# Sliding attention beside a dense block: attention from the last tile to the first, WO blocks in other slots, results turned in place

## The chip, the cores and the metric

The kernel runs on one core of one Trainium2 chip. The metric is the time of one execution on the device in microseconds (us), as the median of several runs. TensorE is PE, VectorE DVE, ScalarE ACT, GpSimd POOL, and SyncE, which here only issues DMAs, SP.

## The reference

One input x of 2048 rows and 576 columns is normed and goes through an attention and a dense block side by side; both are added to x:

```
x  = A_x                                   # 1 x 2048 x 576
xn = layernorm(x)
A: q, k, v = split(xn @ wqkv)              # 32 heads of 18
   key of position s, window place w:  s - 2 w, w = 0..7   (none below 0)
   o = softmax(q . k * 18**-0.5) . v;  o @ wo
B: relu(xn @ w1) @ w2                      # w1 576 x 4608, w2 4608 x 576
out = x + A + B
```

All is float32. Each operand is cut into a high and a low part, and a product is the sum of three partial products.

## The kernel before, in words

**Phases.** The dilation is 2, so even and odd rows never meet. The kernel treats them as two phases (`ph` 0 and 1) of 1024 rows. A partition holds eight consecutive rows of its phase, the tiles 0 to 7 (`NI`): the attention of tile i is that of the i-th row of all 128 partitions.

**The dense block** fills PE. Its first part goes slot by slot (24 slots per phase; slots of phase 1 are counted from 1000): `h_two` makes hidden values, 1.5 us of PE, and `o_two` multiplies them by W2. Its larger part goes by groups (`group`, 30 per phase), in which two by two blocks are multiplied with Strassen's seven products. A group has eight steps; after each step's products (place "T") and after the half output pass behind them (place "O"), `fire` runs what was put at that place by `on(ph, group, step, place, ...)`. The cuts of the weights are such events: `sw_load` and `sw_prep` (W1; A11, S1, ... are its blocks), `w2_load` and `w2_split` (W2), `wq_load` and `wq_split` (the QKV weights). A cut copies the high part on ACT (L172) and subtracts on DVE (L176) or POOL (L174).

**Attention** goes by four units (`u`) of eight heads. `qkv_half` (L488) makes Q, K and V of a unit on PE; ACT puts them into rows of one tile, `att` (L520): Q, K and V each have row numbers there, and V and Q have two places, for even and odd units. `halos` (L527) copies the last seven rows of the partition before to the first seven rows of K and V, by DMAs on SP (L533). `attention` (L542) then queues a list of small jobs: for each tile a product with the window of eight keys (`qk_mul`, L563) and its sum (`qk_sum`, L566), the softmax (`sm_max`, L575, and on), the values (`av_mul`, `av_add`), `o_turn` (L607), which transposes the result block by block, and `o_out`, which writes it to memory with eight DMAs. Tile i reads rows i to i + 7 of K and V; rows 0 to 6 are the halo. After one of the sums POOL masks the places below position 0 (`affine_select`, L569), in partition 0.

**Which job runs when** is settled while the program is written. `run_bg(margin)` (L645) takes jobs from the list as long as the planner's count of DVE time stays within `margin` of its count of PE time. So the jobs stand at fixed places among the cuts and ReLUs on DVE, and each engine takes its instructions in that order.

**WO.** When a phase's last unit is written, `ot_plan` (L1092) says in which order and with which spacing WO is loaded and cut (`wl`, `ws`) and the results are read back and cut (`in`, `split`), on the planner's count of PE time. `wo_block` (L1235) multiplies 256 rows by WO. Block 0 of phase 0 ends `seam`, between the phases; blocks 1 to 3 run in slots 1003, 1006 and 1009 of phase 1, behind `h_two`. Their operands lie in the memory that phase 1's `att` takes over, so phase 1's first `wq_load` (slot 1010) can be issued only when they are through.

**The second phase's x** is normed in phase 0's last slots: `xq_load`, `stats`, `xq_norm`, `turn`, and `blocks_out` (L387, DMAs at L391), which writes the turned tile to memory.

Places in the queue lists: `at(n, ...)` runs in slot n ahead of the output pass, `late(n, ...)` behind it. DMAs on SP go in order of the program.

## Time and profile before

| | us |
|---|---|
| median of 3 runs | 1171.43 (1170.77 to 1171.69) |
| the profiled execution | 1176.77 |
| its span on the core | 1175.0 |
| PE busy | 1125.7 (96%) |
| DVE busy | 816.7 (70%) |
| ACT busy | 562.2 (48%) |
| POOL busy | 472.7 (40%) |

The profile is of one execution. The mean granted PE clock was 0.984 of full speed. A name such as "PE po L163 <- DVE ar L176" says that an instruction of line 163 on PE, which writes tile po, stood idle until DVE's instruction of line 176 on tile ar was done; a line may be that of a helper, so that many places share it. SPq is SP's queue of DMA issues.

### The profile page before, as it was taken

The numbers are of one execution on the slowest core, as the hardware profiler recorded it, in microseconds if no ns is written. First come the engines' busy times: TensorE is split into PE (matmuls) and PEld (weight loads), VectorE is DVE, ScalarE is ACT, GpSimd is POOL, SyncE is SP. The second block draws the span as 40 slices with busy tenths as digits, with TensorE's granted clock in tenths as the row PEclk, the third lists the DMA queues.
The fourth block names the chain that finished last, engine by engine and source line by source line (L and its number), as shares of the span: only waits on it lengthen the run. The fifth ranks groups of instructions, "written<-read, shape, count | busy, mean of one in ns | idle before, by whom it ended". The sixth has DMA issues, their size and how long they took to land.

```text
span 1175.0 us, 38355 instructions
## 1 busy us (share of the span) xinstructions
PE 1125.7 (96%) x16410; PEld 1103.4 (94%) x16410; DVE 816.7 (70%) x1249; ACT 562.2 (48%) x1316; POOL 472.7 (40%) x514
## 2 busy tenths in 40 slices
PE   8999899999999999999997999999999999999996
PEld 8998899999999999998997999999999999999895
DVE  7675788698798788874315438877896886888431
ACT  4443463454355455556534235635644634555540
POOL 2323452353354355553323135434524523555331
PEclk9999899999999999999999999999999999999898
DMA  7479795786697598899947157858858957888984
GB/s 217 156 170 197 139 196 91 142 173 118 141 184 129 98 185 140 156 184 281 189 63 157 24 106 169 157 86 174 173 95 160 204 92 164 143 155 155 215 131 111
DMA packets 159810, 176.82 MB, mean 150 GB/s; under 512 B 36232, under 2 KB 107144, under 8 KB 159608
## 3 DMA queue, kind: packets, MB, share of 16 engines
q0 software_dynamic: 44352, 81.45, 47.5%
q1 hardware_dynamic: 114604, 92.03, 26.8%
q8 instruction: 129, 2.11, 0.7%
q10 hardware_dynamic: 684, 0.88, 0.2%
q14 instruction: 41, 0.34, 0.1%
HBM read 74.07 MB, written 95.70 MB: 144 GB/s over the span
## 4 chain that ended last, share of the span: by engine, by line
PE 73%; DMA 12%; DVE 6%; issue 3%; ACT 3%; SPq 2%; POOL 1%; DVEq 0%; ACTq 0%; POOLq 0%
PE po L163 23%; PE po L142 19%; PE ph L163 12%; PE pm L163 10%; PE pm L142 5%; DMA st<-in_w 4%; DMA out<-ev 3%; PE ph L142 3%; DVE ar L176 2%; DMA att<-od 1%; DMA att<-att 1%; ACT ev L711 1%; DMA xS<-od 1%; DMA od<-pr 1%; DVE ar L757 1%
## 5 line engine op out<-in xcount | busy, mean ns | idle before, releaser
L163 PE MATMUL po<-ar 64*128 64x320 f32 (+1 forms) x5760 | 475.6, 292 | 7.0 <-DVE ar L176 6.3
L163 PEld LDWEIGHTS po<-ar 64*128 64x128 f32 x5760 | 414.9, 186 | 11.3 <-DVE ar L176 9.0
L724 POOL DMA_DIRECT2D out<-ev x256 | 226.6, 1026 | 399.3 <-ACT ev L711 373.0
L163 PE MATMUL ph<-xT,ar 64*128 64x256 f32 x2520 | 328.7, 279 | 15.6 <-ACT pm L975 7.5
L163 PEld LDWEIGHTS ph<-xT,ar 64*128 64x128 f32 x2520 | 291.8, 187 | 21.9 <-ACT pm L975 12.3
L711 ACT ACTIVATE ev<-po 128x512 f32<-128x512 f32 (+1 forms) x268 | 172.8, 650 | 218.2 <-PE po L163 110.4
L163 PE MATMUL pm<-xS,ar 64*128 64x256 f32 x2160 | 267.9, 279 | 1.8 <-ACT u L979 0.7
L163 PEld LDWEIGHTS pm<-xS,ar 64*128 64x128 f32 x2160 | 242.3, 187 | 3.7 <-DVE ar L757 1.1
L176 DVE TENSOR_TENSOR ar<-st,ar 128x256 fp32r<-128x256 f32 (+3 forms) x232 | 146.1, 641 | 64.2 <-ACT ar L172 54.3
L172 ACT ACTIVATE ar<-st 128x256 fp32r<-128x256 f32 (+3 forms) x304 | 147.9, 500 | 21.5 <-DMA st<-in_w 16.2
L174 POOL TENSOR_TENSOR ar<-st,ar 128x256 fp32r<-128x256 f32 (+1 forms) x72 | 94.3, 1323 | 158.6 <-ACT ar L172 156.7
L907 POOL TENSOR_TENSOR st<-st 128x256 f32<-128x256 f32 x120 | 135.9, 1145 | 12.1 <-DMA st<-in_w 7.8
L142 PE MATMUL po<-wq,xT 64*128 64x432 f32 x1296 | 136.4, 353 | 0.0
L142 PEld LDWEIGHTS po<-wq,xT 64*128 64x128 f32 x1296 | 123.6, 184 | 1.5
L163 PE MATMUL ph<-xS,ar 64*128 64x256 f32 x720 | 103.2, 276 | 1.0 <-ACT ph L975 0.8
L563 DVE TENSOR_TENSOR pr<-att 128x1152 f32<-128x1152 f32 x64 | 89.3, 1399 | 18.4 <-DMA att<-att 18.2
L598 DVE TENSOR_TENSOR pr<-att 128x1152 f32<-128x1152 f32 x64 | 89.9, 1423 | 12.2 <-ACT att L520 11.9
L163 PEld LDWEIGHTS ph<-xS,ar 64*128 64x128 f32 x720 | 94.0, 184 | 2.6 <-ACT ph L975 2.0
L566 DVE TENSOR_REDUCE att<-pr 128x64 f32<-128x1152 f32 x64 | 84.9, 1338 | 0.0
L142 PE MATMUL po<-ar 64*128 64x256 f32 (+1 forms) x984 | 73.1, 293 | 2.7 <-ACT ev L711 2.7
L757 DVE SCALAR_TENSOR_TENSOR ar<-u,ar 128x256 fp32r<-128x256 f32 x60 | 31.7, 528 | 63.2 <-ACT ar L753 63.1
L605 DVE TENSOR_TENSOR pr<-pr 128x1152 f32<-128x1152 f32 x64 | 71.5, 1117 | 1.4
(120 smaller groups left out, 1356.4 us busy)
## 6 DMA issues: line engine op xcount, KB each, us to landing
out<-ev POOLq DMA_DIRECT2D x268, 288.0 KB, 6.2
st<-in_w SPq DMA_DIRECT2D x72, 288.0 KB
st<-in_w SPq DMA_DIRECT2D x120, 128.0 KB
att<-att SPq DMA_DIRECT2D x16, 441.0 KB
att<-in_wqkv SPq DMA_DIRECT2D x28, 216.0 KB
od<-pr SPq DMA_DIRECT2D x32, 128.0 KB
att<-in_x SPq DMA_DIRECT2D x14, 288.0 KB
st<-in_w SPq DMA_DIRECT2D x60, 64.0 KB
```

Source lines behind the costliest of these rows:

```text
L142: ins = nc.tensor.matmul(o, l[z], r[z], start=start, stop=stop)
L163: b.ins = nc.tensor.matmul(b.ap, l[part], r[part], start=start, stop=stop, skip_group_check=skip)
L172: nc.scalar.activation(hi, src, AF.Copy)
L174: nc.gpsimd.tensor_tensor(lo, src, f32(hi), op=ALU.subtract)
L176: nc.vector.tensor_tensor(lo, src, f32(hi), op=ALU.subtract)
L563: nc.vector.tensor_tensor(pr[i], q, window(k, i), op=ALU.mult)
L566: nc.vector.tensor_reduce(lg[:, i], pr.pop(i).rearrange(heads, d=Dh), axis=AX.X, op=ALU.add)
L598: nc.vector.tensor_tensor(pr[i].rearrange(heads, d=Dh), e, window(v, i).rearrange(heads, d=Dh), op=ALU.mult)
L605: nc.vector.tensor_tensor(o, z[:, :, 0:n], z[:, :, n : 2 * n], op=ALU.add)
L711: nc.scalar.activation(acc[:, :, cols], z[:, :, 0 : cols.stop - cols.start], AF.Copy)
L724: ADDED[ph, 2 * tb + k] = nc.gpsimd.dma_start(o_v[ph, 2 * tb + k], acc[:, k, :], accum_op=ALU.add)
L907: nc.gpsimd.tensor_tensor(stg(o), stg(a), stg(b), op=op)
```

## The change

Seven things are changed. (1) The products and sums of attention run from tile 7 to tile 0, and the mask follows the sum of tile 0; attention starts one step later. (2) `o_turn` writes into the unit's own V rows and no longer into a scratch tile, and the list isn't held for 5 us behind `o_out` any more; in odd units ACT writes V in an instruction of its own. (3) The cut of A11 moves from step 3 to step 4. (4) WO is cut later behind its load. (5) WO block 1 moves ahead of the hidden pass of its slot, blocks 2 and 3 both ahead of slot 1006, and phase 1's first `wq_load` to slot 1008. (6) `blocks_out` goes behind the loads of its slot, and the statistics, norm and turn of the last two tiles move into groups 0 and 1. (7) Two margins of the list are smaller.

```diff
@@ qkv_half
-            assert len(bg) <= 26, (ph, u, len(bg))
+            assert len(bg) <= 30, (ph, u, len(bg))
...
-            nc.scalar.activation(
-                a[:, q0 + j : q0 + j + 2 * step + 1 : step, :], pq.rearrange("p (s c) -> p s c", s=3), AF.Copy
-            )
+            pq = pq.rearrange("p (s c) -> p s c", s=3)
+            for m, n in ((0, 2), (2, 3)) if u % 2 else ((0, 3),):
+                to = q0 + j + m * step
+                nc.scalar.activation(a[:, to : to + (n - m - 1) * step + 1 : step, :], pq[:, m:n, :], AF.Copy)
@@ attention
         def qk_mul(i):
-            if i % 2 == 0:
+            if i % 2:
                 both = prp.tile([P, 2, W, UD], F32, name="pr")
-                pr[i], pr[i + 1] = both[:, 0], both[:, 1]
+                pr[i], pr[i - 1] = both[:, 0], both[:, 1]
...
-            if i == NI - 2:
+            if i == 0:
                 z = lg[0:1, 0 : NI - 1]
                 nc.gpsimd.affine_select(
...
         def o_turn():
-            z = pr["o"] = prp.tile([P, 5, NI, 32], F32, name="pr")
+            k = V_ROW[u % 2] * UD
+            z = pr["o"] = att(ph)[:, k : k + 5 * NI * 32].rearrange("p (g i e) -> p g i e", g=5, e=32)
...
-            hold["bg"] = t["pe"] + 5.0
...
-        for i in range(0, NI, 2):
+        for j in (NI - 1, NI - 2):
             for f in (qk_mul, qk_sum):
-                for j in (i, i + 1):
+                bg.append((big, f, (j,)))
+        for i in range(NI - 3, 0, -2):
+            for f in (qk_mul, qk_sum):
+                for j in (i, i - 1):
                     bg.append((big, f, (j,)))
@@ run_bg
-        if t["pe"] < hold.get("bg", 0.0):
-            return
@@ plan_strassen
-                on(ph, a - 1, 3, "T", sw_prep, ph, p, "A11")
+                on(ph, a - 1, 4, "T", sw_prep, ph, p, "A11")
...
-            on(ph, g + 2, 2, "O", attention, ph, u)
+            on(ph, g + 2, 3, "O", attention, ph, u)
@@ ot_plan
-            z.append((("ws", kt), wo_split, (ph, kt), None, (("wl", 6 + 1.4 * (kt - 2)),)))
+            z.append((("ws", kt), wo_split, (ph, kt), None, (("wl", 12 + 2.0 * (kt - 2)),)))
...
-            z.append((("in", r), ot_in, (ph, r), free if r == 3 else done, ((("in", r - 1), 5.0),) if r else (("wl", 5.0),)))
+            z.append((("in", r), ot_in, (ph, r), free if r == 3 else done, ((("in", r - 1), 5.0),) if r else (("wl", 6.0),)))
@@ prologue
-        run_bg(1.0)
+        run_bg(0.3)
@@ new
+    def wo_third():
+        EV[0, 3, "wo"] = prp.tile([P, 2, D], F32, name="pr"), []
+        wo_block(0, 3)
@@ phase 0, tiles of the second phase
-                late(n + 1 + odd, do)
                 if i < 6:
+                    late(n + 1 + odd, do)
                     late(n + 2 + odd, xq_norm, i)
                     late(n + 2 + odd, turn, xq(i), 1, i)
-                    at(n + 4, blocks_out, xq(i), 1, i)
+                    late(n + 4, blocks_out, xq(i), 1, i)
                 else:
-                    on(0, 0, 2 + 3 * odd, "O", xq_norm, i)
-                    on(0, 0, 2 + 3 * odd, "O", turn, xq(i), 1, i)
-                    on(0, 0, 7 + odd, "O", blocks_out, xq(i), 1, i)
+                    on(0, 0, 1 + 4 * odd, "O", do)
+                    on(0, 1, 2 + 3 * odd, "O", xq_norm, i)
+                    on(0, 1, 2 + 3 * odd, "O", turn, xq(i), 1, i)
+                    on(0, 1, 5 + 3 * odd, "O", blocks_out, xq(i), 1, i)
@@ phase 1, first slots (first() runs ahead of h_two)
-            for r in range(1, NTB):
-                at(b + 3 * r, wo_block, 0, r)
-            at(b + 10, wq_load, ph, 0)
+            first(b + 3, wo_block, 0, 1)
+            first(b + 6, wo_block, 0, 2)
+            first(b + 6, wo_third)
+            at(b + 8, wq_load, ph, 0)
...
-        late(b + UNIT0[ph] + NI + 1, attention, ph, 0)
+        late(b + UNIT0[ph] + NI + 2, attention, ph, 0)
@@ slots
-            run_bg(margin(n))
+            run_bg(margin(n) - (1.4 if n == b + NOLD - 4 else 0.0))
```

More of the change, by code (lines that the diff above doesn't have):

```diff
@@ L1343, in at, with first @@
         todo.setdefault(n, []).append((f, a))
+    todo_first = {}
+    def first(n, f, *a):
+        todo_first.setdefault(n, []).append((f, a))
     todo_late = {}
@@ L1521, in tile_body @@
             g = n - n % 2 + LAG
+            for f, a in todo_first.pop(n, []):
+                f(*a)
             if n < ROW0:
```

## The prediction

> **What bounds the kernel now.** The page comes first: which engine fills the span.
>
> ```profile
> span 1175.0 us, 38355 instructions
> PE 1125.7 (96%) x16410; PEld 1103.4 (94%) x16410; DVE 816.7 (70%) x1249; ACT 562.2 (48%) x1316; POOL 472.7 (40%) x514
> ```
>
> PE is the bound: it is busy for all but 49.3 us. The edits keep the matrix work; both built programs hold the same matmuls, DVE, POOL and DMA instructions, and ACT alone has 32 more. A gain can come only from PE's idle time and from the half-clock stretches behind it. So the second view is who PE waited for (total us, times, longest):
>
> ```profile
> PE ph L163 <- ACT pm L975: 7.5, 14, 1.8
> PE po L163 <- DVE ar L176: 6.3, 7, 1.6
> PE pm L142 <- ACT wq L172: 6.0, 1, 6.0
> PE ph L163 <- DVE ar L176: 5.5, 3, 4.8
> PE po L142 <- ACT ev L711: 2.7, 4, 1.3
> ```
>
> No releaser is slow by itself: the rows below show copies and splits of 0.4 to 0.6 us. Something holds its queue. The third view cuts the span around each stall (window, length, busy us of PE, PEld, DVE, ACT, POOL, then granted clock, DMA share, GB/s):
>
> ```profile
> 108.00:116.00 8.00, 7.07 (x102) 6.36 (x99) 4.22 (x5) 4.59 (x11) 3.17 (x4) 1.00 0.99 169
> 116.00:120.67 4.67, 0.00 (x2) 0.01 (x2) 3.57 (x11) 0.00 (x0) 2.38 (x4) 0.68 0.36 113
> 120.67:126.00 5.33, 5.11 (x47) 4.65 (x47) 3.60 (x7) 1.19 (x3) 2.56 (x4) 0.64 1.07 178
> 223.00:226.70 3.70, 1.84 (x24) 1.33 (x22) 3.70 (x5) 0.87 (x3) 0.44 (x1) 1.00 0.87 162
> 226.70:232.00 5.30, 5.30 (x66) 5.30 (x64) 4.64 (x8) 2.47 (x7) 1.78 (x2) 0.68 0.69 145
> 320.00:322.20 2.20, 1.63 (x21) 1.10 (x19) 2.20 (x4) 0.66 (x2) 0.42 (x1) 1.00 0.96 145
> 415.00:418.00 3.00, 1.30 (x15) 0.80 (x14) 3.00 (x5) 0.92 (x3) 0.95 (x1) 1.00 0.99 179
> 418.00:423.00 5.00, 5.00 (x60) 5.00 (x60) 4.44 (x7) 2.41 (x6) 1.68 (x2) 0.66 0.99 266
> 526.00:531.00 5.00, 2.82 (x36) 2.24 (x36) 3.14 (x5) 3.57 (x8) 1.96 (x3) 0.97 1.09 304
> 531.00:536.00 5.00, 5.00 (x62) 5.00 (x62) 1.27 (x3) 2.94 (x7) 2.24 (x3) 0.69 1.12 253
> 638.00:644.16 6.16, 0.17 (x2) 0.00 (x0) 2.20 (x5) 1.28 (x4) 0.00 (x0) 0.94 0.82 188
> 644.16:652.00 7.84, 7.84 (x69) 7.55 (x71) 7.38 (x13) 3.04 (x7) 1.97 (x2) 0.62 0.15 42
> 700.00:706.00 6.00, 4.78 (x61) 3.88 (x60) 5.03 (x8) 2.27 (x7) 2.86 (x4) 1.00 0.95 163
> 803.00:805.00 2.00, 0.91 (x11) 0.39 (x7) 2.00 (x4) 0.47 (x2) 0.41 (x1) 1.00 0.98 165
> 989.00:992.00 3.00, 1.30 (x16) 0.78 (x14) 3.00 (x5) 0.66 (x2) 1.22 (x1) 1.00 0.90 153
> 1100.00:1105.00 5.00, 2.51 (x30) 1.85 (x28) 3.09 (x5) 4.09 (x9) 1.77 (x2) 0.92 1.07 305
> 1105.00:1112.00 7.00, 7.00 (x72) 7.00 (x74) 2.56 (x6) 3.46 (x8) 2.64 (x3) 0.57 1.11 269
> ```
>
> Read them in pairs. A stall costs its idle time (length less PE busy) and then the work lost at the lower clock, (1 - clock) x length of the row behind it. Six stalls have a half-clock stretch behind them: the rows at 120.67, 226.70, 418, 531, 644.16 and 1105.
>
> **The change part by part**, each with the price of the stall that it touches.
>
> *Statistics of the second half, and the order on SP.* The DVE row shows the wait in brackets, the SP row the queue ahead of the load:
>
> ```profile
> 103.18 9.96 SPq L391 DMA_DIRECT2D words<-att  x8
> 116.96 0.82 DVE L303 BATCH_NORM_STATS2 bst<-att 128x6 f32<-128x288 f32 x2 [4.75 <-DMA att<-in_x]
> ```
>
> Eight block writes stood ahead of the load of x tiles 6 and 7, DVE waited 4.75 us for it, and the weight splits behind waited too. Now the loads go ahead of the block writes, and the statistics move into groups 0 and 1, behind those splits. The loads can be issued from 103.18 on, no longer behind 103.18 + 9.96 = 113.14; with the 3.8 us to landing seen before (116.96 - 113.14) they are there well ahead of 116. The 5.60 us idle in the first two windows and (1 - 0.64) x 5.33 = 1.92 go: 7.5. Late next are the splits of A22 and the remainder, about due when PE arrives; I keep 0.5 of cost there. Gain **7.0**.
>
> *Attention from the last tile, one step later.* Tile 7's window covers rows 7 to 14, its partition's own; the halo fills rows 0 to 6. In the changed program the first product waits for no DMA, the second for the halo. Before, the first one waited:
>
> ```profile
> 217.13 3.21 SPq L533 DMA_DIRECT2D att<-att  x4
> 222.75 1.92 DVE L563 TENSOR_TENSOR pr<-att 128x1152 f32<-128x1152 f32 x1 [3.94 <-DMA att<-att]
> 224.59 0.81 DVE L176 TENSOR_TENSOR ar<-st,ar 128x256 fp32r<-128x256 f32 x2
> ```
>
> The second split of L176, that of W2, held up PE at 223; the same happened at 320, 415, 803 and 989. In the new order it precedes attention. The second product comes about four and a half steps after the halo's issue, at the code's STEP of 1.46 us some 6.5 us; the halo took 222.75 - 217.13 = 5.6. Idle: 1.86 + 0.57 + 1.70 + 1.09 + 1.70 = 6.92; clock: 0.32 x 5.30 + 0.34 x 5.00 = 3.40. Of 10.3 I take **9.5**.
>
> *The seam.* WO blocks 2 and 3 now run back to back ahead of slot 1006, and the next QKV weights are issued in slot 1008 and no longer 1010. Their memory is free only when the last WO block is through, so SP waited for it.
>
> ```profile
> 575.43 1.53 PE pm L142 x26
> 576.97 1.59 PE po L142 x24
> ```
>
> The first row is one hidden pass, the second one output pass: together a slot of 3.1 us. WO block 3 moves from inside slot 1009 to ahead of slot 1006, past three slots and one hidden pass: 10.8 us earlier. The rows behind it were these:
>
> ```profile
> 624.36 2.58 SPq L229 DMA_DIRECT2D att<-in_wqkv  x4
> 630.06 0.86 SPq L207 DMA_DIRECT2D st<-in_w  x1
> 642.88 0.78 ACT L172 ACTIVATE ar<-st 128x256 fp32r<-128x256 f32 x2 [6.97 <-DMA st<-in_w]
> ```
>
> ACT waited for the W2 block issued at 630.06 behind that load, 12.8 us to landing, and the last two splits of QKV weights stood behind ACT. With block 3 10.8 us earlier the weight load meets an emptier queue, and the W2 block follows alone, as soon as its buffer is free. PE stood from 638 on, so to be harmless it must land by about 637, 6 us sooner than before. The stall is 5.99 idle and 0.38 x 7.84 = 2.98 of clock: 9.0, of which I take **8.0**. The three waits of about 0.45 behind the blocks (2.7 - 1.3 in the list) have a hidden pass between block and next tile now; but blocks 1 and 2 start right behind an eviction. I take **0.6** of 1.4.
>
> *WO splits later (12 instead of 6 us behind the load), the result transposed sooner, in place.* ACT took the splits in order while their data was still landing, from the second phase's chain:
>
> ```profile
> 1095.61 7.95 DMA att<-wo
> ```
>
> The last part landed at 1103.56; with the turn two steps earlier (step 3 for 5) its issue moves up by perhaps 1.5 us, and the splits come 5 to 6.5 us later. Idle 2.18 + 2.49, clock 0.31 x 5.00 + 0.43 x 7.00 = 4.56: 9.2 in both phases. ACT may instead wait for the W2 block that now stands behind the eight result writes. I take **7.5**. In place costs nothing on DVE: both transposes run on DVE behind the last reader of those rows.
>
> *Less attention in the last slots.* The DVE products ahead of a due ReLU cost PE 1.22 in the window at 700. I take **0.7**.
>
> Sum of gains: 7.0 + 9.5 + 8.0 + 0.6 + 7.5 + 0.7 = **33.3** of 38.6 on the table.
>
> *What is added.* The mask of the first rows now follows the last logits directly, and the maximum waits for it. The cost rows (group, count, busy us, mean ns):
>
> ```profile
> L569 POOL TENSOR_SCALAR_AFFINE_SELECT att<-att 1x448 f32<-1x448 f32 x8 | 8.3, 1041 | 4.6 <-DVE att L566 4.5
> L566 DVE TENSOR_REDUCE att<-pr 128x64 f32<-128x1152 f32 x64 | 84.9, 1338 | 0.0
> L520 ACT ACTIVATE att<-po 128x432 f32<-128x432 f32 x48 | 22.9, 529 | 72.9 <-PE po L142 72.9
> L979 ACT ACTIVATE u<-pm 128x256 f32<-128x256 f32 x60 | 23.0, 384 | 38.0 <-PE pm L163 38.0
> L724 POOL DMA_DIRECT2D out<-ev x256 | 226.6, 1026 | 399.3 <-ACT ev L711 373.0 <-ACT u L979 14.2 <-ACT ar L753 10.2
> ```
>
> Before, a sum of 1.34 us covered the mask's 1.04. Now other splits and ReLU lows stand between in seven units of eight. Queued behind the maximum are ReLU lows and splits, for which PE waits. Bounds: 0, and 8 x 1.04 = 8.3; I take 1.0, since most of the cover is left. The eviction of odd units is two instructions instead of one, 32 more: bounded by 0 below and by a whole 256-column copy each (0.38) above, 12.3; ACT is 48% busy and waits for PE ahead of L520, so 0.5. In steps 3 of odd groups a sum or the transposes now stand ahead of the W2 split, where the A11 split stood: 1.34 - 0.41 = 0.9 later, at ten places, with about three steps until PE reads it. Bounds 0 and 9.3; I take 2.0, near the first. The seam's queue: 1.0. Added: **4.5**.
>
> Net 33.3 - 4.5 = 28.8. The profiled execution took 1176.77 (span 1175.0 and 1.8 around it), so it would be 1148; the median of the runs shown is 1171.43, 5.3 below, and I put the same 28.8 there: **1143**.
>
> [...]
>
> **The rivals.**
> 1. *The clock drops are not the short stalls' doing.* For it: the row at 989. Against: the four short stalls that have one behind them. Then 1.70 + 1.70 + 1.55 + 3.01 = 8.0 stays: 1151. [...] Chance 0.05.
> 2. *The seam's wait stays:* the W2 block still lands after PE, since result writes fill the queues. For it: 12.8 us to landing before; against: the load ahead is issued 10.8 us sooner. 8.0 back: 1151. Chance 0.13.
> 3. *The WO weights are still late,* since their writes wait for the result writes. 7.5 back: 1150. Chance 0.12.
> 4. *The halo wait only moves to the second product* (the edit doesn't do what it says); 1 us of margin. 9.5 back: 1152. Chance 0.08.
> 5. *DVE becomes the bound at the mask:* POOL's queue is in order, and the mask stands behind two accumulating writes (2 x 1.03) and its own 1.04. If that is 3.1 us of DVE wait in each unit, long enough to pass on to PE with its clock (3.1 + 1.7), eight units cost 38.4; with the other 3.5 added and 33.3 gained that is 8.6 more: **1180**, slower. It decides when DVE's slack at the maximum is under about 1 us. Against: the list of PE's waits names DVE's splits and ACT, and no long wait behind POOL. Chance 0.05.
>
> **How the numbers follow.** The forecast has 0.57. Everything gained and nothing added gives 1171.4 - 38.6 = 1133; two rivals at once give some 1159. Range **1131 to 1158**: it leaves out rival 5 and pairs of rivals beyond 1158. Of rivals 1 to 4 all are faster by over 0.2% (2.3 us, about what a measurement of this kernel can tell from no change). Faster 0.93, same 0.02, slower 0.05.
>
> **What would show it.** Right: no DMA wait of the first product, PE wait on "ACT wq" gone or under 1 us, no stretch of half clock but at the end; PE busy falling with the half-clock stretches, by about 12 us. Wrong: a new DVE wait for POOL at the maximum; ACT waiting for "st<-in_w" near 630; W2 splits named as PE's releaser in odd groups; a total of PE idle time over 30 us.

## The result, and the profile after

| | before | changed |
|---|---|---|
| first runs, median us | 1171.56 (1170.77 to 1174.45) | 1160.06 (1158.69 to 1162.36) |
| ratio, with its 95% interval | | 0.9899 (0.9876 to 0.9923) |
| two later sets of runs, ratio | | 0.9936 (0.9913 to 0.9959), 0.9935 (0.9904 to 0.9966) |

The changed kernel is faster by 9 to 11.5 us of median (11.50, 9.03 and 10.42 in the three sets), where 28.8 were forecast; 1160 lies just above the forecast's range. The profiled execution took 1158.69 us. First the page after, span and engines:

```profile
span 1156.9 us, 38381 instructions
...
PE 1116.8 (97%) x16410; PEld 1094.4 (95%) x16410; DVE 814.3 (70%) x1249; ACT 560.3 (48%) x1348; POOL 469.5 (41%) x514
```

PE is still the bound; it was idle for 40.1 us (49.3 before), so the prediction's sign of being wrong, "a total of PE idle time over 30 us", came true. Then what PE waited for (us in all, times, longest):

```profile
PE ph L163 <- ACT ph L977: 9.1, 6, 3.8
PE ph L163 <- ACT pm L977: 7.2, 12, 0.9
PE ph L142 <- ACT xT L422: 2.2, 1, 2.2
```

The two rows that named DVE's splits (6.3 and 5.5) and the seam's "ACT wq" of 6.0 are gone. At the top stands L977, `seed`: ACT's copy of a finished sum into the PSUM bank that the next product adds to (L975 before). Its row on pm was there before (7.5); new is the one on ph, 9.1 where it was 0.8. ACT does it late, because something stands ahead of it in ACT's order. What, two stretches show. First ACT at the end of the first phase (start, us, then in brackets the idle time before and what ended it):

```profile
523.18 0.74 ACT L674 ACTIVATE att<-att 128x640 fp32r<-128x640 f32 x1 [2.53 <-DMA att<-od]
525.75 0.60 ACT L713 ACTIVATE ev<-po 128x512 f32<-128x512 f32 x1 [1.83 <-DMA out<-ev]
526.25 0.41 ACT L755 ACTIVATE ar<-u 128x256 fp32r<-128x256 f32 x1
...
527.17 0.72 ACT L674 ACTIVATE att<-att 128x640 fp32r<-128x640 f32 x1
527.79 0.37 ACT L977 ACTIVATE ph<-ph 128x256 f32<-128x256 f32 x1
```

The cut of the attention result waits for its read-back, the eviction behind it for the accumulating write that still reads its buffer, and the seed, which needs neither, comes last: PE stood 3.78 us. Second, DVE in a steady group, with the 0.9 us stall at 149.6 behind it:

```profile
144.66 1.35 DVE L564 TENSOR_TENSOR pr<-att 128x1152 f32<-128x1152 f32 x1
145.93 1.34 DVE L567 TENSOR_REDUCE att<-pr 128x64 f32<-128x1152 f32 x1
147.19 0.55 DVE L176 TENSOR_TENSOR ar<-st,ar 128x320 fp32r<-128x320 f32 x1
147.66 1.13 DVE L176 TENSOR_TENSOR wq<-att,wq 128x432 fp32r<-128x432 f32 x1
148.71 0.41 DVE L759 SCALAR_TENSOR_TENSOR ar<-pm,ar 128x256 fp32r<-128x256 f32 x1
```

An attention product and a sum of 1.3 us each, then two weight cuts; the ReLU low (L759), which frees the bank for the seed, is fifth.

### The profile page after: what moved, and what is told of

It is laid out like the page before. It is cut to its first block, busy times and chain, and to the rows that moved or that the text cites. A ratio compares the mean times of both kernels' runs of the same rounds, so it can differ in the third digit from the quotient of the medians.

```text
span 1156.9 us, 38381 instructions
## 1 busy us (share of the span) xinstructions
PE 1116.8 (97%) x16410; PEld 1094.4 (95%) x16410; DVE 814.3 (70%) x1249; ACT 560.3 (48%) x1348; POOL 469.5 (41%) x514
## 3 DMA queue, kind: packets, MB, share of 16 engines
q0 software_dynamic: 44352, 81.45, 46.8%
q1 hardware_dynamic: 114604, 92.03, 27.3%
## 4 chain that ended last, share of the span: by engine, by line
PE 74%; DMA 10%; DVE 5%; ACT 4%; issue 3%; POOL 1%; SPq 1%; ACTq 0%; DVEq 0%; POOLq 0%
PE po L163 23%; PE po L142 19%; PE ph L163 12%; PE pm L163 9%; PE pm L142 5%; DMA out<-ev 4%; PE ph L142 3%; DMA att<-od 2%; ACT ev L713 1%; PE ph L130 1%; DVE ar L759 1%; DVE ar L176 1%; PE po L130 1%; DVE wq L176 1%; DMA xS<-out 1%
## 5 line engine op out<-in xcount | busy, mean ns | idle before, releaser
L163 PE MATMUL po<-ar 64*128 64x320 f32 (+1 forms) x5760 | 469.2, 291 | 1.5 <-ACT ev L713 1.0
L163 PEld LDWEIGHTS po<-ar 64*128 64x128 f32 x5760 | 410.3, 185 | 4.1 <-ACT ev L713 1.6
L163 PE MATMUL ph<-xT,ar 64*128 64x256 f32 x2520 | 323.5, 277 | 10.0 <-ACT pm L977 7.2
L163 PEld LDWEIGHTS ph<-xT,ar 64*128 64x128 f32 x2520 | 287.4, 185 | 15.5 <-ACT pm L977 10.3
L163 PE MATMUL pm<-xS,ar 64*128 64x256 f32 x2160 | 261.1, 276 | 1.3 <-ACT u L981 0.6
L163 PEld LDWEIGHTS pm<-xS,ar 64*128 64x128 f32 x2160 | 236.9, 184 | 2.9 <-ACT u L981 1.3
L176 DVE TENSOR_TENSOR ar<-st,ar 128x256 fp32r<-128x256 f32 (+3 forms) x232 | 148.8, 646 | 87.5 <-ACT ar L172 76.4
L172 ACT ACTIVATE ar<-st 128x256 fp32r<-128x256 f32 (+3 forms) x304 | 148.6, 503 | 15.2 <-DMA st<-in_w 11.5
L909 POOL TENSOR_TENSOR st<-st 128x256 f32<-128x256 f32 x120 | 130.0, 1096 | 12.1 <-DMA st<-in_w 7.7
L142 PEld LDWEIGHTS po<-wq,xT 64*128 64x128 f32 x1296 | 120.2, 184 | 2.6
L599 DVE TENSOR_TENSOR pr<-att 128x1152 f32<-128x1152 f32 x64 | 87.5, 1380 | 0.4
L564 DVE TENSOR_TENSOR pr<-att 128x1152 f32<-128x1152 f32 x64 | 86.4, 1351 | 0.2
L567 DVE TENSOR_REDUCE att<-pr 128x64 f32<-128x1152 f32 x64 | 85.2, 1339 | 0.0
L759 DVE SCALAR_TENSOR_TENSOR ar<-u,ar 128x256 fp32r<-128x256 f32 x60 | 29.8, 497 | 68.5 <-ACT ar L755 68.4
## 6 DMA issues: line engine op xcount, KB each, us to landing
st<-in_w SPq DMA_DIRECT2D x120, 128.0 KB
od<-att SPq DMA_DIRECT2D x32, 128.0 KB
```

Of the source, the lines that this page charges most:

```text
L142: ins = nc.tensor.matmul(o, l[z], r[z], start=start, stop=stop)
L163: b.ins = nc.tensor.matmul(b.ap, l[part], r[part], start=start, stop=stop, skip_group_check=skip)
L172: nc.scalar.activation(hi, src, AF.Copy)
L176: nc.vector.tensor_tensor(lo, src, f32(hi), op=ALU.subtract)
L564: nc.vector.tensor_tensor(pr[i], q, window(k, i), op=ALU.mult)
L567: nc.vector.tensor_reduce(lg[:, i], pr.pop(i).rearrange(heads, d=Dh), axis=AX.X, op=ALU.add)
```

## The experiments

Runs of one kernel spread over several us, so the comparisons go by the ratio to runs of the kernel before on the same chip, and the mechanisms by profiles.

| kernel | median us | ratio to before (95%) |
|---|---|---|
| changed, later sets | 1162.16; 1160.34 | 0.9936; 0.9935 (above) |
| `u_sp` | 1168.27 | 0.9985 (0.9969 to 1.0000) |
| `b_sp` | 1165.43 | 0.9942 (0.9922 to 0.9961) |
| `u_seam` | 1166.11 | 0.9952 (0.9926 to 0.9978) |
| `u_attn` | 1164.16 | 0.9937 (0.9913 to 0.9961) |
| `u_turn` | 1160.18 | 0.9874 (0.9852 to 0.9895) |
| `u_attn_turn`, twice | 1157.36; 1154.91 | 0.9868 (0.9849 to 0.9887); 0.9882 (0.9850 to 0.9913) |
| `b_ev` | 1166.79 | 0.9974 (0.9947 to 1.0001) |
| `u_ot` | 1163.37 | 0.9898 (0.9875 to 0.9921) |
| `splate` | 1161.32 | 0.9892 (0.9870 to 0.9914) |
| `evp1`; `evp2` | 1160.20; 1158.39 | 0.9884 (0.9863 to 0.9906); 0.9880 (0.9860 to 0.9899) |
| `last_scratch` | 1162.08 | 0.9896 (0.9866 to 0.9926) |
| `best1`; `best2` | 1158.00; 1160.30 | 0.9896 (0.9866 to 0.9927); 0.9888 (0.9863 to 0.9914) |

### Second profiles of both kernels

> The kernel before, unchanged, for a second profile. Theory A (the forecast counted its gains on one execution that was 5.3 us slower than the median, and some of its stalls are not there in a usual one): the span comes out 3 to 7 us shorter than the first profile's 1175.0, and one or more of the priced stalls (4.79 at 120, 1.62 at 225, 1.47 at 416, 1.81 at 530, 6.00 at 644, 1.47 at 990, 1.34 at 1102) are shorter by 0.5 us or lack the half clock behind them. Rival B (the stalls are the same in every execution, and the difference lies elsewhere): the span is 1174 to 1176 with the same stalls within 0.3 us.

> The changed kernel, unchanged, for a second profile and a narrower interval. Theory A (the gain is given back at the end of the first half of the rows, where ScalarE waits in order for read-backs and result writes ahead of the seed that TensorE needs): 0.988 to 0.991 of before, and the second profile shows TensorE idle again 3 to 4 us near 528 and 2 us near 544, and 2 to 3 us near 1097. Rival C (those waits are an accident of the one profiled execution): they are under 1.5 us this time, or sit elsewhere.

> The changed kernel again, on the same chip as the next. Theory A: 0.988 to 0.994 of before, stalls of 2 us or more near 528 and 1097 in the profile.

The second execution of the kernel before took 1167.32 us, 9.5 less than the one that the forecast was worked out from. Its waits of PE:

```profile
PE ph L163 <- ACT pm L975: 9.9, 15, 2.6
PE po L163 <- DVE ar L176: 6.6, 7, 1.7
...
PE pm L142 <- ACT wq L172: 0.9, 1, 0.9
```

The seam's wait is 0.9 us, not 6.0; the DVE stalls of 1.5 to 1.7 us are all there again. Theory A holds, with a span shorter by more than its 3 to 7 us, and which stalls are steady can be told. For the changed kernel, C falls: the stall at the end of the first phase came again with 2.98 and 8.04 us, that of the second with 7.33 and 2.98. The ratio of the second set, 0.9936, is also above the 0.988 to 0.991 that theory A gave.

To set whole stretches against each other, each span is cut at the same seeds (the 3rd, 9th, 81st, 91st and 20 us, 93rd, 169th, 182nd and 6 us). Busy time of PE, PEld, DVE, ACT, POOL, then granted clock; the second profile of before:

```profile
114.00:142.40 28.40, 23.65 (x320) 22.06 (x318) 17.95 (x35) 11.46 (x28) 11.19 (x13) 0.88 0.70 139
142.40:501.30 358.90, 352.30 (x5272) 347.52 (x5270) 296.31 (x404) 183.71 (x441) 164.50 (x174) 1.00 0.76 147
501.30:559.40 58.10, 54.15 (x825) 51.74 (x825) 31.75 (x59) 36.04 (x84) 25.45 (x29) 1.00 1.03 241
559.40:689.00 129.60, 125.55 (x1858) 123.44 (x1858) 44.91 (x82) 50.25 (x109) 35.66 (x39) 1.00 0.56 106
689.00:1057.50 368.50, 361.39 (x5435) 356.94 (x5432) 301.97 (x414) 189.00 (x455) 170.70 (x180) 1.00 0.76 148
1057.50:1114.90 57.40, 54.08 (x848) 53.19 (x845) 37.96 (x67) 35.39 (x82) 24.05 (x26) 0.97 0.94 190
```

The changed kernel, first profile:

```profile
112.60:134.90 22.30, 21.02 (x318) 19.62 (x316) 17.51 (x34) 11.15 (x28) 11.72 (x13) 1.00 0.85 162
134.90:491.80 356.90, 350.90 (x5273) 345.77 (x5271) 294.85 (x406) 182.86 (x457) 161.87 (x174) 1.00 0.77 148
491.80:552.80 61.00, 54.62 (x800) 52.81 (x797) 30.85 (x56) 34.25 (x80) 24.41 (x28) 0.94 1.02 231
552.80:680.80 128.00, 126.41 (x1884) 124.27 (x1882) 45.76 (x86) 52.10 (x114) 37.04 (x41) 1.00 0.57 107
680.80:1048.80 368.00, 361.98 (x5435) 355.55 (x5431) 302.20 (x414) 188.46 (x471) 166.77 (x180) 1.00 0.76 148
1048.80:1105.50 56.70, 52.13 (x837) 51.13 (x837) 36.99 (x65) 34.05 (x80) 23.73 (x26) 1.00 0.92 190
```

The lengths of these stretches in all profiles of three kernels, and the difference of the means of the first two columns:

| stretch | before | changed | `u_attn_turn` | changed less before | forecast |
|---|---|---|---|---|---|
| last x tiles | 28.0, 28.4 | 22.3, 22.6, 22.4 | 22.6, 22.5 | -5.8 | -7.0 |
| groups, first phase | 361.4, 358.9 | 356.9, 356.3, 356.0 | 356.9, 356.1 | -3.8 | together -6.7 |
| groups, second phase | 368.6, 368.5 | 368.0, 370.4, 369.1 | 370.0, 368.2 | +0.6 | |
| end of first phase | 59.3, 58.1 | 61.0, 60.7, 64.7 | 59.6, 59.6 | +3.4 | together -7.5 |
| end of second phase | 58.7, 57.4 | 56.7, 61.5, 56.5 | 54.3, 54.0 | +0.2 | |
| seam and slots | 135.0, 129.6 | 128.0, 130.7, 125.6 | 125.1, 127.4 | -4.2 | -7.6 |

The forecast column sorts its terms: 9.5 + 0.7 less the additions of 1.0, 0.5 and 2.0 for the groups, 8.6 - 1.0 for the seam. The stretches ahead of and behind these changed by -1.0 and +0.7. The mean spans differ by 9.8: 28.8 less 11.1 lost at the ends, 3.5 in the groups, 3.4 at the seam and 1.0 elsewhere.

### The x tiles and the order on SP

`u_sp` puts the statistics and block writes back in their old places; `b_sp` is the kernel before with only this part changed:

```diff
@@ b_sp
-                late(n + 1 + odd, do)
                 if i < 6:
+                    late(n + 1 + odd, do)
...
-                    at(n + 4, blocks_out, xq(i), 1, i)
+                    late(n + 4, blocks_out, xq(i), 1, i)
                 else:
-                    on(0, 0, 2 + 3 * odd, "O", xq_norm, i)
-                    on(0, 0, 2 + 3 * odd, "O", turn, xq(i), 1, i)
-                    on(0, 0, 7 + odd, "O", blocks_out, xq(i), 1, i)
+                    on(0, 0, 1 + 4 * odd, "O", do)
+                    on(0, 1, 2 + 3 * odd, "O", xq_norm, i)
+                    on(0, 1, 2 + 3 * odd, "O", turn, xq(i), 1, i)
+                    on(0, 1, 5 + 3 * odd, "O", blocks_out, xq(i), 1, i)
```

> The changed kernel with the statistics of the second half's last two tiles and the block writes in their old slots. Theory A (the step was worth what the seeds' distance shows in the two profiles, 5.9 us, against 7.0 forecast): 5 to 6.5 us slower than the changed kernel, 0.994 to 0.996 of before, with the load at 103 behind eight block writes again. Rival B (that stall is small outside the first profile): under 3 us slower, 0.989 to 0.992.

> The kernel before with the first part of the change alone: the statistics of the second half's last two tiles in the first two groups, the block writes behind the loads. Theory A (this step alone is worth most of the change's net gain; the other parts together came to 1.7 us in the run without it): 5 to 7 us faster than before, 0.994 to 0.996. Rival H (it frees only time that the later stalls take back): under 2 us, 0.998 or more.

In both theory A had the difference: `u_sp` is 6.1 us of median slower than the changed kernel on its chip. Its ratio to before, 0.9985, is above A's 0.994 to 0.996, because the changed kernel itself was at 0.9936 there. Alone this part gives 0.58% (6.8 us), and without it the changed kernel is only 0.15% faster than before. The stretch is 30.6 us in `u_sp` and 22.8 in `b_sp`.

### The seam

```diff
-            first(b + 3, wo_block, 0, 1)
-            first(b + 6, wo_block, 0, 2)
-            first(b + 6, wo_third)
-            at(b + 8, wq_load, ph, 0)
+            for r in range(1, NTB):
+                at(b + 3 * r, wo_block, 0, r)
+            at(b + 10, wq_load, ph, 0)
```

> The changed kernel with the WO blocks and the QKV load of the seam in their old slots. In the second profile of before the wait for the QKV split there was 0.9 us, in the first 6.0. Theory A (the 6.0 was one execution's, the step is worth about what the second profile shows): 0 to 3 us slower than the changed kernel, 0.991 to 0.995 of before, with 0.9 to 3 us of wait behind the QKV split near 635 and 0.45 us behind each block. Rival B (6.0 is usual): 6 to 8 us slower, 0.996 to 0.999.

The wait came back, in this profile with

```profile
PE pm L142 <- ACT wq L172: 4.5, 1, 4.5
```

The five profiled executions with the old seam had 6.00, 0.88, 4.49, 2.70 and 2.19 us of it. With the new seam no profile has it; a wait for DVE's cut of the QKV weights is at most 0.6 us there, but PE waits 0.6 to 2.3 us for a ReLU low near 624. The seam's stretch is 130.7 us on average in these five and 127.9 in the other fifteen profiles: 2.8 us. The ratio lies between the two theories' numbers, and nearer to A.

### The attention's order, the result's place, the split eviction

`u_attn` sets the order of the tiles, the start, the A11 cut and the two margins of the list back; `u_turn` the scratch tile and the pause; `u_attn_turn` both (parts of the edits):

```diff
@@ u_attn
-        for j in (NI - 1, NI - 2):
+        for i in range(0, NI, 2):
...
-            on(ph, g + 2, 3, "O", attention, ph, u)
+            on(ph, g + 2, 2, "O", attention, ph, u)
...
-        run_bg(0.3)
+        run_bg(1.0)
@@ u_turn
-            k = V_ROW[u % 2] * UD
-            z = pr["o"] = att(ph)[:, k : k + 5 * NI * 32].rearrange("p (g i e) -> p g i e", g=5, e=32)
+            z = pr["o"] = prp.tile([P, 5, NI, 32], F32, name="pr")
...
+            hold["bg"] = t["pe"] + 5.0
```

`b_ev` is the kernel before with one edit:

```diff
-            nc.scalar.activation(
-                a[:, q0 + j : q0 + j + 2 * step + 1 : step, :], pq.rearrange("p (s c) -> p s c", s=3), AF.Copy
-            )
+            pq = pq.rearrange("p (s c) -> p s c", s=3)
+            for m, n in ((0, 2), (2, 3)) if u % 2 else ((0, 3),):
+                to = q0 + j + m * step
+                nc.scalar.activation(a[:, to : to + (n - m - 1) * step + 1 : step, :], pq[:, m:n, :], AF.Copy)
```

> The changed kernel with the attention in its old order again: first tile first, one step sooner, the A11 mix back in its step. Theory A (the halo step was priced about right, some 7 us net of what it adds): 5 to 8 us slower than the changed kernel, 0.994 to 0.997 of before, with the first product waiting 3 to 4 us for the halo and TensorE standing at 223, 415 and 990 again. Rival C (the new order adds as much as it takes, by the 0.9 us waits of the seed behind product, sum and splits): within 2 us of the changed kernel, 0.988 to 0.992.

> The changed kernel with the turned result in the scratch tile and the 5 us pause of the attention queue again. Theory A (the halo's wait has two cures, either alone is enough: the new order of the tiles, or the result writes issued sooner): no first product waits over 1 us for the halo, no stall at 223, 416 and 990, within 2.5 us of the changed kernel, 0.989 to 0.995 of before. Rival E (the sooner writes alone cured it): the stalls come back under the new order too, 4 to 7 us slower, 0.995 to 0.999.

> The changed kernel with the attention in its old order and the turned result in the scratch tile with its pause: both cures of the halo's wait undone. Theory A (either cure is enough, so each alone cost nothing to undo, and both together cost what the step was worth): the first product waits 3 to 4.5 us again, TensorE stands 1.5 us near 218, 408 and 983, the groups of the first half take 3 to 4 us longer than in the changed kernel, mostly at half clock; 3 to 6 us slower than the changed kernel in all, 0.994 to 0.997 of before. Rival C (the stalls do not come back, or cost nothing): within 2 us, 0.989 to 0.993.

> The kernel before with the split eviction of the odd units alone. Theory A (in the kernel before, the value products of the even units wait 11.9 us in all for evictions of the odd unit, whose one strided write spans their rows without touching them; split, they don't wait, the turned result goes out some 4 us sooner and its eight writes are off the queue when the halo's copies are issued): no wait of the value products for ScalarE, the halo's wait falls from 3.9, 3.5 and 3.4 us near 223, 414 and 988 to under 2.6, two or three of the stalls there go; 2 to 6 us faster than before, 0.995 to 0.998. Rival J (the forecast's view: it only adds 32 instructions): 0 to 1 us slower, 1.000 to 1.001.

> The changed kernel with both attention parts undone, again, on the same chip as the changed kernel. Theory A (the reversal and the in-place result cost more than they bring, since the split eviction has already cured the halo's wait): 2 to 5 us faster than the changed kernel here. Rival K (the 2.8 us between their medians was the difference between chips): within 1.5 us.

The first surprise was `u_attn`: the old order, and no stall behind DVE's W2 split at 225, 416 or 990 (the 1.3 us near 417 end with a seed). Its ratio, 0.9937, is that of the changed kernel on the same chip, as theory C had the difference. I took the result writes, now sooner, for a second cure. With both cures undone the stalls had to return, and that run refuted it: `u_attn_turn`, faster than both its theories, was the fastest kernel. What was left of the change in its attention was the split eviction. DVE's waits in the kernel before had a row for it:

```profile
DVE pr L563 <- DMA att<-att: 18.2, 6, 3.9
...
DVE pr L598 <- ACT att L520: 11.9, 8, 2.5
```

L598 multiplies the weights by the values of an even unit, in rows 38 to 52. L520 writes Q, K and V of the next, odd unit with one access of step 30: rows 0 to 7, 30 to 37 and 60 to 67. They share no row, but the write's span runs over the values, and the product waited. With V in an instruction of its own the row for L598 is gone, and the halo's wait in `b_ev` is down:

```profile
DVE pr L564 <- DMA att<-att: 11.2, 6, 2.2
```

This is theory A. The stalls at 225 and 416 are gone, PE idle in the groups falls from 6.6 to 5.5 us in the first phase and from 7.1 to 4.3 in the second (against the second profile of before), and the median by 4.0 us (the interval just includes no change). On the queue the reason can be read. SP's last result write before:

```profile
216.59 0.44 SPq L622 DMA_DIRECT2D od<-pr  x1
```

The halo's row there, at 217.13, followed it at once. In `b_ev` SP has finished the eight result writes when the halo is due:

```profile
213.48 0.46 SPq L623 DMA_DIRECT2D od<-pr  x1
216.71 3.18 SPq L534 DMA_DIRECT2D att<-att  x4
```

There are 2.8 us between them. So the reversed order removed a wait that another edit of the same change had already shortened enough: in `u_attn` the first product still waits 1.5 to 2.3 us, but no stall of PE of that kind follows. The order also went with more of the 0.5 to 0.9 us waits behind L564 and L567: such waits in the groups add up to 8.5 us in the changed kernel's first profile and to 3.8 in `u_attn`. On one chip the changed kernel ran 1159.31 to 1164.66 and `u_attn_turn` 1153.19 to 1158.99: undoing both parts gains 5.4 us of median, and no run of one reaches those of the other; rival K falls, and it is a little more than theory A had. `u_turn` (0.9874) against `u_attn` (0.9937), each against before on its own chip, says that the larger part of this is the place of the result and its pause, not the order; `u_turn` came out faster than either theory had it.

### The ends of the phases

`splate` delays the cuts of the read-back, `evp1` gives the last two groups two more eviction buffers, `evp2` has both, `u_ot` has the planner's old gaps (6 + 1.4 and 5.0 for 12 + 2.0 and 6.0):

```diff
-                z.append((("split", r, h), ot_split, (ph, r, h), None, ((("in", r), 9.0 if ph or r == 0 else 22.0),)))
+                z.append((("split", r, h), ot_split, (ph, r, h), None, ((("in", r), 16.0 if r == 0 else 14.0 if ph else 22.0),)))
@@ group
+        if g == NG - 2:
+            z = prp.tile([P, 2, 2, D], F32, name="pr")
+            EV[ph, 3, "o"], EV[ph, 2, "o"] = (z[:, 0], []), (z[:, 1], [])
```

> The changed kernel with the splits of the read-back result due later: 16 for 9 us behind the read of the first block, 14 for 9 behind the others in the second half, so that ScalarE has both seeds of the step in front of them. Theory A (ScalarE waits for the read-back, 2.5 us in one profile and 8.0 in the other, ahead of the seed): TensorE's stalls near 528 and 1097 to 1105 fall under 1.5 us each, that near 545 shrinks with them, since the loads behind wait for the same queue; 5 to 10 us faster than the changed kernel, 0.982 to 0.988 of before. Rival F (the eviction on the same engine waits for its buffer's accumulating write anyway, until 525.75 in the first profile): 2 to 4 us stay at each place, under 2.5 us faster, 0.988 to 0.993.

> The changed kernel with two more eviction buffers in the last two groups, in the scratch tile that the turned result no longer uses; nothing else moved. Theory A (two things hold ScalarE ahead of the seed near 528 and 1097: the eviction that waits for its buffer's accumulating write, and the split that waits for the read-back): the eviction's wait goes, the split's of 2.5 to 8 us stays; the stalls keep 2 to 6 us; 0.987 to 0.992 of before, within 2.5 us of the changed kernel. Rival F (the buffer alone decides): stalls under 1.5 us, 0.982 to 0.987.

> The same two buffers and the later splits of the read-back result together. Theory A: both waits gone, the stalls near 528 and 1097 under 1 us each and the half clock behind them with them; TensorE's waits at the end of the first half (6.3 and 9.0 us in the two profiles) under 4, of the second (4.3 and 7.3) under 2; 0.981 to 0.987 of before. Rival G (the transfers themselves are the limit: whichever copy next needs data waits instead, so the loss only changes its place): 5 us or more stay at the first end, 3 at the second; 0.987 to 0.992.

> The changed kernel with the planner's old gaps for the WO splits and the read-back (6 + 1.4 and 5.0 for 12 + 2.0 and 6.0). Theory A (the stall near 528 and 1100 is the first split of the read-back result, which stands on ScalarE ahead of the seed whatever the WO splits do): the stalls stay, 2 to 6 us each in the profile, some of it behind the WO data instead; 0.989 to 0.995 of before, within 2.5 us of the changed kernel. Rival D (the new gaps make the stall): both under 1.5 us, 4 us or more faster than the changed kernel, 0.984 to 0.989.

With `splate` alone the eviction waits instead (4.5 us at 525.0, 4.3 at 1095.0), as rival F had it; with `evp1` alone the cut (3.4 and 6.0), as theory A had it. With both, the second end is cured (52.2 us, PE idle 0.9), but at the first ACT next waits for W2 of the other phase:

```profile
531.66 0.77 ACT L172 ACTIVATE ar<-st 128x256 fp32r<-128x256 f32 x2 [7.18 <-DMA st<-in_w]
```

In `u_ot` it waits 6.5 us for WO at 518.8 instead, as theory A had it. So for `evp2` G is right at the first end, where WO, result, and x and weights of the next phase all load, and A at the second. In the windows above the DMA share at the first end is 1.02 to 1.03, in `evp2` it is 1.00: the packets' times add up to all the time of the 16 engines.

Why the changed kernel is worse here than `u_attn_turn` is partly to be read on SP. In place, WO's memory is also what the result writes read. The changed kernel's SP at the second end:

```profile
1075.98 0.43 SPq L624 DMA_DIRECT2D od<-att  x1
1077.04 0.36 SPq L207 DMA_DIRECT2D st<-in_w  x1
1079.19 0.86 SPq L257 DMA_DIRECT2D att<-wo  x2
1080.10 1.14 SPq L260 DMA_DIRECT2D att<-wo  x2
1081.29 0.58 SPq L207 DMA_DIRECT2D st<-in_w  x1
1081.91 0.43 SPq L395 DMA_DIRECT2D att<-od  x1
```

and that of `u_attn_turn`, second run:

```profile
1074.78 0.45 SPq L623 DMA_DIRECT2D od<-pr  x1
1075.29 1.09 SPq L257 DMA_DIRECT2D att<-wo  x2
...
1078.36 0.84 SPq L395 DMA_DIRECT2D att<-od  x1
```

From the last result write to the first read-back it is 5.9 us there and 3.6 here. In three profiles of the changed kernel the cut waited 2.5, 2.7 and 8.0, and 8.7 and 2.0 us for the read-back (one end had none); in two of `u_attn_turn` never. Also, W2's load (1077.04) now stands behind the result writes; in `u_attn_turn` it is ahead of them. The last unit's place alone was then tried:

```diff
-            z = pr["o"] = att(ph)[:, k : k + 5 * NI * 32].rearrange("p (g i e) -> p g i e", g=5, e=32)
+            z = att(ph)[:, k : k + 5 * NI * 32].rearrange("p (g i e) -> p g i e", g=5, e=32)
+            if u == NU - 1:
+                z = prp.tile([P, 5, NI, 32], F32, name="pr")
+            pr["o"] = z
```

> The changed kernel with one thing undone: the last unit's turned result of each half goes to the scratch tile; the others stay in place, and there is no pause. Theory L (in place makes the WO loads and the read-backs, which take over the memory of those rows, wait until the eight result writes have landed, 2 to 3 us, and the split of the read-back then holds ScalarE ahead of the seed; it matters for the last unit alone): the first read-back is issued 3.4 to 4.7 us behind the last result write and not 4.8 to 8, the split waits under 2 us in both ends, 3 to 6 us faster than the changed kernel, 0.986 to 0.989 of before. Rival M (the pause, or the other units' place, is what made the run with the old place faster): within 1.5 us of the changed kernel, 0.991 to 0.994.

The read-back came 5.0 and 4.6 us behind the last write, and the cut waited 0.4 and 2.2: shorter, as L had it, though one number of each pair is outside L's bounds. The time is between the two theories and tells neither; the eviction's wait (3.2 and 1.8 us) kept the stalls at 3.1 and 3.4. How much of the 5.4 us is the place, the pause or W2's load stays open.

### What is left

> Both attention parts undone, with the two more eviction buffers and the later splits of the read-back result. Theory A (the parts add up): 1 to 4 us faster than the kernel with both attention parts undone alone, 0.980 to 0.986 of before, TensorE's waits at the two ends under 4 and 2 us. Rival G (the transfers are the limit at the ends): within 1.5 us of it.

> The kernel before with three parts of the change: the statistics and the order on the load queue, the seam, the split eviction; attention order, place of the turned result and the planner's gaps as before. Theory A (the later WO splits only exchange a wait of ScalarE for WO data against others at the same place): within 2 us of the kernel with both attention parts undone, 0.986 to 0.990 of before, with ScalarE waiting 4 to 6 us for WO data near 518 and 1086. Rival D (the gaps are worth the 4 us or more that the forecast gave them): 3 to 6 us slower than it, 0.991 to 0.994.

`best1` doesn't beat `u_attn_turn`: its median on the same chip is 3.1 us longer, which neither theory had, though the runs of the two overlap. At the second end PE is idle for 0.2 us, but 2.9 come back at 1135, where WO's last block waits for a cut. `best2`, without the later gaps for WO, has ACT waiting 4.3 and 4.8 us for WO, and its ratio, 0.9888, is in theory A's range; its median (1160.3) is one of another chip. The fastest version found is `u_attn_turn`: the change without the new order, place and margins. `u_turn`, with the new order, can't be told from it (0.9874 against 0.9868 and 0.9882).

## Why the prediction was wrong, by its own steps

Of the 19.0 us by which the spans missed the forecast, 11.1 were lost at the ends of the phases: the term "WO splits later, the result transposed sooner, in place" is the step that failed most. The attention's term is the second that failed, by its mechanism; the seam's was mis-sized.

- **What bounds:** right. Span less PE idle and half-clock loss is 1106 to 1110 us in the first two profiles of both kernels. But the sum took an execution 5.3 us slower than the median as a set of steady stalls, 12.9 us of half clock among them. By windows of 2 us, half-clock loss was 19.3 us in it and 11.7 in the second. And the idle time of its window rows adds up several waits: where the rows at 223, 415, 526 and 1100 have 1.70 to 2.49 us, the longest single ones are 1.34 to 1.81.
- **Statistics and order on SP:** right: 7.0 forecast, 5.8 by the stretch, 6.8 alone.
- **Attention from the last tile:** the halo's waits went as said. The step that failed is the one after: 9.5 was priced as if nothing else touched that stall and nothing took its place. The split eviction had all but ended it, and product and sum, moved ahead of the ReLU low, gave much back: waits of 0.5 to 1.0 us in the groups add up to 5.5 in the second profile of before (0.9 of it a priced stall) and to 7.9 to 8.5 in the three of the changed kernel. 2.0 were set for that. PE idle in the groups of both phases was 13.3 and 13.5 us before and 11.7, 13.5 and 12.9 changed, where 6.9 were to go.
- **"The eviction of odd units is two instructions instead of one ... bounded by 0 below":** wrong in sign, as far as 4.0 us of median whose interval just includes no change can tell. It was priced by what the instruction costs on ACT and not by who waits for it. The page's group of L598 had 11.9 us of idle behind L520.
- **The seam:** right mechanism, mis-sized: 8.6 from a wait of 6.0, which ranges from 0.9 to 6.0; 2.8 to 4.2 measured.
- **WO and the turn:** 7.5 forecast, 3.6 lost at the two ends. ACT's wait for WO did go. "ACT may instead wait for the W2 block that now stands behind the eight result writes" did happen (4.32 us at 1083.81 in the changed kernel, 1.2 of it passed on to PE), but was given no price, and "In place costs nothing on DVE" asked only DVE: the place is also memory that SP's next loads wait for (L257, WO's load, waited 2.7 us in all for the result writes in the changed kernel's first profile). At the first end of the changed kernel's first profile ACT waited 2.5 us for the read-back and 1.8 for the buffer, and PE stood 3.8; how the loss divides between place, pause and W2's load stays open. Rival 3 named late WO; late were the read-back and the eviction buffer, whose instructions stood ahead of the seed in ACT's order.
- **Mask and maximum:** 1.0 forecast. DVE waits for POOL at the maximum once in the changed kernel, 1.3 us, and not in seven of the eight units; what of it reached PE is not shown.

## What to carry to other kernels

Take two profiles of the kernel before, and price only stalls that both show, and half clock only where both show it: behind the stall near 225 the first profile of before has 3.41 us of it, the second none. For an edit that splits or moves an instruction, look up in the groups who is idle behind it before bounding its cost at nothing below. At the first end, at a DMA share of 1.00, `evp2` took two waits of ACT away and the next transfer showed behind them, with 7.18 us: in such a stretch price the whole and not the stall.

## What the runs showed of the hardware

In every profile the half-clock stretches begin on one grid of 3.41 us (at 117.71, 226.94, 418.08, 530.72, 643.36 and 1104.16 in the first of before, whole multiples apart), which lies elsewhere in each execution (a window of it begins at 226.94 in the first of before, at 225.88 in the second), and, but for the one that the end of the span cuts off, last 3.4, 6.8 or 10.2 us. At the granted clock of 0.50 that is, as an estimate, 1.7, 3.4 or 5.1 us of work. Cut the span on that grid, and the stall near 225 reads so in the first profile of before, then in the second, then that at 1097 in the changed kernel (clock third from the end):

```profile
223.52:226.94 3.42, 1.56 (x20) 1.05 (x18) 3.42 (x6) 1.11 (x4) 0.00 (x0) 1.00 0.97 181
226.94:230.35 3.41, 3.41 (x34) 3.41 (x32) 3.41 (x6) 1.92 (x6) 0.35 (x1) 0.50 0.72 194
222.47:225.88 3.41, 2.11 (x36) 1.85 (x32) 1.78 (x3) 0.00 (x0) 1.72 (x3) 1.00 0.99 169
225.88:229.29 3.41, 2.81 (x40) 2.55 (x42) 3.41 (x5) 2.63 (x7) 0.00 (x0) 1.00 1.02 250
229.29:232.70 3.41, 3.41 (x64) 3.41 (x62) 3.03 (x7) 1.70 (x5) 1.78 (x2) 1.00 0.67 119
1092.15:1095.57 3.42, 2.26 (x34) 2.02 (x31) 0.63 (x2) 0.85 (x3) 0.00 (x0) 1.00 1.11 254
1095.57:1098.98 3.41, 1.80 (x30) 1.80 (x32) 2.90 (x7) 3.41 (x10) 0.94 (x2) 1.00 1.09 284
1098.98:1102.39 3.41, 3.41 (x59) 3.41 (x58) 2.38 (x5) 2.18 (x6) 0.81 (x1) 1.00 1.10 199
```

In the first the whole stall fell into one window: 1.86 us of idle, and half clock in the next. In the second nearly the same stall lay across two (1.30 and 0.60), and the 2.77 us at 1097 did too (1.16 and 1.61): no drop. Of the windows at full clock in the 20 profiles, the first and last 12 us of each span left out, 37 had over 1.83 us of PE idle and half clock followed each; 6537 had less than 1.64 and it followed none; of the 17 between, it followed nine. So of these three stalls the 1.86 us in one window had a drop behind them, the 1.90 and the 2.77 us across two had none. What makes the clock drop is not shown.

The accumulating writes took more DMA time per byte than the rest. From 505 to 515 in the changed kernel (queue: packets, MB, share of 16 engines):

```profile
q0 software_dynamic: 449, 0.90, 64.6%
q1 hardware_dynamic: 1029, 1.27, 37.2%
```

The first row's queue carries them (its out<-ev and out<-pr, 276 x 288 KB, are 81.4 of its 81.45 MB over the whole span): 10 x 16 x 0.646 / 0.90 = 115 us of one engine per MB, against 47 for the loads and plain writes. Over the whole span (81.45 MB at 46.8%, 92.03 at 27.3%) it is 106 against 55. No run tells whether it is the adding or the queue that costs.
